# Softmax attention mixed with a spectral filter: a smaller third transform and a newly made order of work

## The chip, the cores and the metric

One core of a Trainium2 chip runs the whole program. The metric is the device time of one execution in microseconds (us). The engines are named TensorE (PE in the profile), VectorE (DVE), ScalarE (ACT), GpSimd (POOL) and SyncE (SP, which here only issues transfers).

## The reference

A token matrix x of 2048 x 448 goes through two branches, whose results are mixed by a gate of one number per token.

```python
g = sigmoid((x * gate_w).sum(-1, keepdims=True))
# branch a: 16 heads of 28
q, k, v = split(x @ wqkv)
a = softmax(q @ k.T / sqrt(28)) @ v @ wo
# branch b: a spectral filter over both axes
X = rfft2(x)                       # 2048 x 225 complex
b = irfft2(X * (w_r + 1j * w_i), s=(2048, 448))
out = g * a + (1 - g) * b
```

## The kernel before

**The stream of attention.** Heads are worked in 4 groups of 4, tokens of a group's queries in 4 blocks of 512: 16 chunks (`CHUNKS`). In each chunk 16 key tiles of 128 make a *pack* each: four score blocks of 128 x 512, one for each head, 1024 in all. A score block is one matmul on a strip of 32 rows of TensorE (`Emit.score`), so up to four run at once; the text calls such a group of concurrent matmuls a *cell*. ScalarE takes score blocks in pairs, from the two-bank tiles psA and psB in turn (`Emit.exp`, one ACTIVATE of 128 x 1024). VectorE takes whole packs from single banks psX: it makes the exponential's bit pattern with integer arithmetic, once (`bits`) and three times shifted (`shift`). Value cells (`value`) add into psV, four column strips of 32.

**The spectral branch** is done with matrix products beside the stream: `fft1` (over 128 token residues, result U), then `fft2`, which for each of 16 groups g does a second transform along the features (f2, result P2), a third one over the 16 remaining token steps (f3, result FX; its tables come by transfer into `tab`), the multiplication with the filter on GpSimd (the filter's rows come by transfer into Wf), and the first inverse one (i1). `fft3` and `final` finish it and add the output projection. A complex product in f3 is, before the change, one pass of 452 columns and two of 226 on full 128 partitions:

```python
self.mmc(bank[:, 0:452], tb[:, 0:128], p2[:, :], True, False)
self.mmc(bank[:, 0:226], tb[:, 128:256], p2[:, 226:452], False, False)
self.mmc(bank[:, 226:452], tb[:, 256:384], p2[:, 0:226], False, True)
```

`mmc` splits a product into four column strips of 32, which run at once.

**The order of the work** is written by a planner in the kernel itself (`Plan`), when the program is built. Each operation has an engine, a duration, dependencies and a priority; units of TensorE work have a place (`at`) and a due time in units of progress of the stream. The planner walks through time, takes for each engine the best operation that is ready, and puts out one list; each engine's queue is that list in order, and an engine waits at an instruction until what it depends on is done. `CFG` holds the weights, with own values for each of 72 stretches of progress (`seg`). `m_pe` and `m_bank` are reserves that the plan leaves between another engine's end and TensorE's start, and before a bank is used again. No duration in it is taken at run time. When TensorE has too little work the planner puts in cells on zeros (`zero`).

**The head** (`head`, `first`) transposes x block by block (xT, L1267 and L1274), projects the first key and query blocks, squares them on ScalarE (sq, L1302), adds a norm row by one matmul, and copies KT and QT (L1311, one KT copy at L1309 on ScalarE). Then the first scores are possible. The minimum of KT (`kmin`, L1277) is needed later, for a bound that the softmax uses in place of a maximum. **The tail** (`norm_last`, `final`) normalises the last chunk from psV on VectorE and finishes the last output tiles.

Of the kernel before, what the change touches and what calls it, by code (L numbers as in the profile page):

```python
# [18 lines left out]
FP = F + 1  # L19
# [22 lines left out]
def rfft_tables():  # L42
# [42 lines left out]
    tab = np.concatenate([CR, -CI, CI, CRt, -CIt, CIt, CRt, 0 * CR], axis=2)  # L85
# [32 lines left out]
class Op:  # L118
# [4 lines left out]
    passes = 1  # L123

# [40 lines left out]
class Plan:  # L165
# [152 lines left out]
    def step(self, eng, t):  # L318
# [7 lines left out]
        prog = self.progress()  # L326
        for o in lst:
            if o.start is not None:
                continue
            if o.ready > t:  # L330
                continue
# [149 lines left out]
    def tile_ready(self, tl):  # L481

        r = tl["ready"]
        for b in self.bank_of[tl["grp"]]:
            if self.owner[b] is not None and self.owner[b] != "stream":
                return None
            if not self.started or self.owner[b] is None:
                r = max(r, self.free_at[b])
        e = self.last_exp[tl["grp"]]
        if e is not None:  # L490
            if e.get("end") is None:
                return None
            r = max(r, e["end"] + self.cfg["l_pe"])
        return r
# [8 lines left out]
    def exp_dur(self, n):  # L503
        return 512 * n * 0.000833 + 0.055
# [14 lines left out]
    def exp_run(self, e, t):  # L519
# [3 lines left out]
        self.done(o, t, t + d + 0.11, t + d, "ACT")  # L523
# [84 lines left out]
    def d_sums(self, d):  # L608
# [16 lines left out]
        for v in range(1, 4):  # L625
            eng = "POOL" if (self.nd, v) in self.cfg["pool_shifts"] or (v == 1 and self.cfg["pool_every"] and self.nd % self.cfg["pool_every"] == 0) else "DVE"
            o = Op(eng, self.cfg["dve_shift"] if eng == "DVE" else self.cfg["pool_shift"],
                   (lambda e, v=v: self.em.shift(d["vslot"][v], d["slot"], v, e)), list(d["ops"]),
                   port=True, prio=self.cfg["prio_shift"], name="shift")
# [16 lines left out]
    def pe_step(self, t):  # L646
# [14 lines left out]
        def offer(score, kind, n, go, eff=1.0):  # L661
# [20 lines left out]
        for u in self.open:  # L682
            if u.pos < len(u.pe):
                o = u.pe[u.pos]
                if o.nwait == 0 and o.ready <= t:
                    offer(c["w_open"] - (c["w_due"] if u.due < prog else 0.0) - u.rush, o.kind, o.n, lambda u=u, o=o: self.unit_run(u, o, t), o.eff)
# [5 lines left out]
        if fb:  # L692
            nopen = ndue = 0
            for u in self.todo:
                if u.at > prog:
                    break
                if early and not u.rush:
                    continue
                o = u.pe[0]
                if o.nwait == 0 and o.ready <= t:  # L700
                    if u.due < prog:
                        ndue += 1
                    offer(c["w_new"] - (prog - u.at) * c["w_late"] - (c["w_due"] if u.due < prog else 0.0) - u.rush, o.kind, o.n, lambda u=u, o=o: self.unit_open(u, o, fb[-1], t), o.eff)
# [23 lines left out]
    def zero(self, t, kind, bank):  # L727
# [4 lines left out]
        x.emit = lambda: self.em.zero(kind, bank, first)  # L732
# [17 lines left out]
    def s_run(self, tl, t):  # L750
# [29 lines left out]
        while n > 0 and fb:  # L780
# [8 lines left out]
            n -= 1  # L789
        return True  # L790
# [55 lines left out]
    def unit_run(self, u, o, t):  # L846
# [8 lines left out]
    port_dep=6.0, last=((0, 2), (2, 2)), x_act=4, tiles=(2, 2), nring=20, nvar=10, nearly=5, l_pe=0.09, l_act=0.03, pe_lat=0.2, dma_issue=0.6,  # L855
    m_pe=0.2, m_bank=0.1, tol=0.1, max_ahead=9, nd_max=99, d_open=3, ahead=3, d_chunks=1, dve_op1=0.605, dve_shift=0.6, pool_shift=2.0,
    pool_shifts=(), pool_every=0, prio_op1=3, prio_shift=2.5, sh_max=4, d_urg=2, window=3.413, z_hard=3450, z_soft=3500, v2_at=2.0, v2_due=2.8,
    g_at=(0.9, 4.3, 8.0), g_due=1.0, w_pv=1.0, w_open=0.5, w_new=1.6, w_late=0.5, w_d=3, w_due=2, hungry=1.4, v_rush=2, x_rush=6, k_rush=5, q_rush=4,
    w_hungry=1, sw_pen=0, pv_min=1, ring_urg=2, d_first=True,
    seg={  # L860
        0: dict(d_open=4, w_hungry=0, z_hard=3550, w_open=1.2, tol=0.15),
        1: dict(d_open=4, w_hungry=0, z_hard=3550, w_open=1.2),
        2: dict(d_open=4, w_hungry=0, z_hard=3550, w_open=1.2, w_d=0.5, pv_min=2, tol=0),
        3: dict(d_open=4, w_hungry=0, z_hard=3550, w_open=1.2, w_due=4, z_soft=3800),
        4: dict(tol=0, d_open=2, prio_shift=3.5, z_hard=3350, d_urg=3, z_soft=4200),
        5: dict(tol=0, d_open=2, sw_pen=0.5, d_urg=0),
        6: dict(d_open=2),
        7: dict(d_open=2, w_d=2.2),
        8: dict(d_urg=3, pv_min=2, tol=0.06),
        9: dict(d_urg=3, pv_min=2, tol=0.06, z_hard=3350, d_chunks=0),  # L870
        10: dict(d_urg=3, pv_min=2, tol=0.06, w_due=1),
        11: dict(w_hungry=4),
        12: dict(tol=0.15, g_due=0.8, w_hungry=4, z_hard=3550),
        13: dict(tol=0.15, g_due=0.8, w_hungry=4, z_hard=3550, prio_shift=3),
        14: dict(tol=0.15, g_due=0.8, w_hungry=4, z_hard=3550, prio_shift=3, sw_pen=0.25),
        15: dict(tol=0.15, g_due=0.8, w_hungry=0, z_hard=3550, sw_pen=0.25, d_first=False, pv_min=3, hungry=1),
        16: dict(ahead=1, tol=0.15, g_due=0.8, w_hungry=0, z_hard=3550, sw_pen=0.25, d_first=False, pv_min=3, hungry=1, d_open=4),
        17: dict(ahead=2, tol=0.15, g_due=0.8, w_hungry=0, z_hard=3550, d_first=False, pv_min=3, hungry=1, prio_shift=3.5),
        18: dict(ahead=2, tol=0.15, g_due=0.8, w_hungry=0, z_hard=3550, d_first=False, pv_min=3, hungry=1, w_d=1, max_ahead=5),
        19: dict(ahead=2, tol=0.15, g_due=0.8, w_hungry=0, z_hard=3550, d_first=False, pv_min=3),  # L880
        20: dict(v2_due=3.1, w_pv=0.6, tol=0.15, g_due=0.8, w_hungry=0, z_hard=3550),
        21: dict(v2_due=3.1, hungry=4, w_pv=0.6, tol=0.15, g_due=0.8, w_hungry=0, d_first=False, d_open=4),
        22: dict(v2_due=3.1, hungry=4, w_pv=0.6, tol=0.15, g_due=0.8, w_hungry=0, d_first=False, d_open=4, ring_urg=8),
        23: dict(v2_due=3.1, hungry=4, w_pv=0.6, tol=0.15, g_due=0.8, w_hungry=4, prio_shift=3.5),
        24: dict(hungry=4, prio_shift=3.5, tol=0.15, g_due=0.8, w_hungry=0, w_due=4),
        25: dict(hungry=4, prio_shift=3.5, tol=0.15, g_due=0.8, w_hungry=0, w_due=4, d_open=2),
        26: dict(hungry=4, prio_shift=3.5, tol=0.06, g_due=0.8, w_hungry=0, w_due=4, d_open=2, sh_max=2),
        27: dict(hungry=4, prio_shift=3.5, tol=0.15, g_due=0.8, w_hungry=0, w_due=0.5, d_open=2, d_urg=3),
        28: dict(g_due=0.8, w_hungry=0, prio_shift=3.5, w_due=4, d_open=2, z_soft=4200, d_first=False),
        29: dict(g_due=0.8, w_hungry=0, prio_shift=3.5, w_due=4, d_open=2, z_soft=4200, d_first=False, sh_max=3),  # L890
        30: dict(g_due=0.8, w_hungry=0, prio_shift=3.5, w_due=4, z_soft=4200, d_first=False, sh_max=3),
        31: dict(g_due=0.8, prio_shift=3.5, w_due=4, w_hungry=0, z_soft=4200, d_first=False, sh_max=3, sw_pen=0.5, hungry=1),
        32: dict(g_due=0.8, prio_shift=3.5, w_due=4, w_hungry=2, z_soft=4200, d_first=False, sh_max=3, sw_pen=0.5, hungry=1),
        33: dict(g_due=0.8, prio_shift=3.5, z_soft=4200, d_first=False, sh_max=3, sw_pen=0.5, hungry=1, w_hungry=2, tol=0.06),
        34: dict(g_due=0.8, prio_shift=3.5, z_soft=4200, d_first=False, sh_max=3, w_hungry=0, d_urg=0, ahead=4),
        35: dict(g_due=0.8, prio_shift=3.5, z_soft=4200, d_first=False, w_hungry=2, d_urg=3),
        36: dict(d_urg=3, d_chunks=0, w_due=4, prio_shift=3.5, z_hard=3550, z_soft=4200, g_due=0.8, ring_urg=4, d_first=False, w_hungry=2),
        37: dict(d_urg=3, d_chunks=0, w_due=4, prio_shift=3.5, z_hard=3550, g_due=0.8, w_d=2.2),
        38: dict(d_urg=3, d_chunks=0, w_due=0.5, prio_shift=3.5, z_hard=3550, g_due=0.8, w_d=1.4, w_hungry=2),
        39: dict(d_urg=3, d_chunks=0, w_due=4, prio_shift=3.5, z_hard=3550, g_due=0.8, sh_max=3, pv_min=2, w_d=2.2, hungry=3),  # L900
        40: dict(prio_shift=3.5, d_urg=1, sh_max=3, pv_min=2, w_d=2.2, hungry=3),
        41: dict(prio_shift=3.5, d_urg=1, sh_max=3, pv_min=2, w_d=2.2, hungry=3, w_due=4, ring_urg=8, sw_pen=1),
        42: dict(prio_shift=3.5, d_urg=1, sh_max=3, pv_min=2, hungry=3, w_d=2.2),
        43: dict(d_urg=3, sh_max=3, pv_min=2, d_first=False, hungry=3, w_d=2.2),
        44: dict(d_urg=1, w_d=2.2, pv_min=2, z_soft=4200, z_hard=3250, w_late=1),
# [784 lines left out]
```

## Time and profile before

| | |
|---|---|
| median of 3 runs | 395.97 us (395.78 to 396.46) |
| the profiled execution | 396.53 us, of which its span from first to last instruction 394.4 us |
| granted TensorE clock, mean | 0.999 |
| TensorE busy | 382.2 us (97%), 5432 matmuls |
| ScalarE busy | 380.8 us (97%) |
| VectorE busy | 353.3 us (90%) |
| GpSimd busy | 131.2 us (33%) |
| transfers | 17.57 MB, mean 45 GB/s |

Busy time counts a record from its start to its end; records of one engine can overlap, and an instruction's record may hold its wait behind the one ahead. The time from one start to the next is therefore often the better price. A timeline row is: start in us, duration in us, engine, line, operation, output<-input, shapes, count, and in brackets the idle time before it and what ended that. A row of groups is: line, engine, operation, output<-input, shapes, count | busy us, mean ns of one | idle us before them. A row of the waits is: engine, output, line <- what it waited for: us in total, times, longest us.

### The profile page before, as it was taken

The page shows a single profiled execution, that of the slowest core. Times are in us where ns is not written, and L with a number is a line of the kernel's source. Part 1 is how long each engine was busy: PE and PEld are TensorE (multiplying, and loading weights), DVE is VectorE, ACT ScalarE, POOL GpSimd, SP SyncE. Part 2 cuts the span into 40 slices and gives each one's busy share as a digit, 9 for nine tenths or more (in the row PEclk, how much of TensorE's full clock was granted, in tenths as well). Part 3 has the DMA queues.
Part 4 walks back from the last instruction along what each step waited for, and adds up shares of the span by engine and source line. Part 5 has one row for each costly group of instructions (what it writes and reads, how often), then busy time and mean ns, then how long its engine had stood idle before and what let it go on. Part 6 is the DMA issues. An engine that isn't in the chain of part 4 may idle for free.

```text
span 394.4 us, 13102 instructions
## 1 busy us (share of the span) xinstructions
PE 382.2 (97%) x5432; PEld 134.9 (34%) x5432; DVE 353.3 (90%) x651; ACT 380.8 (97%) x421; POOL 131.2 (33%) x180
## 2 busy tenths in 40 slices
PE   7999999999999999999999999999999999999996
PEld 3544333223333333333433233332233333233333
DVE  3658989899899889989999899999999999999993
ACT  4899999999999999999999999999999999999994
POOL 3130513530530434553555254362343543001010
PEclk9999999999999999999999999999999999999999
DMA  8800012010201202121131200231010101010012
GB/s 243 180 29 5 4 18 56 16 30 3 62 12 47 55 9 67 41 59 50 28 84 40 69 3 30 67 87 38 3 28 3 31 2 30 24 51 27 27 52 71
DMA packets 24411, 17.57 MB, mean 45 GB/s; under 512 B 15731, under 2 KB 19872, under 8 KB 24352
## 3 DMA queue, kind: packets, MB, share of 16 engines
q1 hardware_dynamic: 23744, 16.55, 15.4%
q8 instruction: 42, 0.69, 0.7%
q10 hardware_dynamic: 608, 0.19, 0.3%
q14 instruction: 17, 0.14, 0.1%
HBM read 14.57 MB, written 1.97 MB: 42 GB/s over the span
## 4 chain that ended last, share of the span: by engine, by line
PE 59%; ACT 33%; issue 5%; DMA 1%; DVE 0%; SPq 0%; ACTq 0%
ACT P L963 30%; PE psX L1014 20%; PE psV L1014 18%; PE psA L1014 10%; PE psB L1014 10%; DMA xtok<-in_A_x_dram 1%; ACT VS L963 1%; ACT sq L1636 0%; PE psX L1267 0%; ACT sq L1302 0%; ACT xT L1274 0%; SPq L1169 0%; DVE KT L1311 0%; DVE QT L1311 0%; PE psV L1267 0%
## 5 line engine op out<-in xcount | busy, mean ns | idle before, releaser
L963 ACT ACTIVATE P<-psB 128x1024 bf16<-128x1024 f32 x196 | 218.4, 1114 | 0.3
L963 ACT ACTIVATE P<-psA 128x1024 bf16<-128x1024 f32 x196 | 217.8, 1111 | 0.3 <-ACT P L963 0.2
L992 DVE TENSOR_SCALAR VS<-psX 128x512 int16<-128x512 f32 x220 | 144.0, 683 | 10.6 <-PE psX L1014 9.7
L998 DVE TENSOR_SCALAR VS<-VS 128x2048 int16<-128x2048 int16 x165 | 107.5, 694 | 0.5
L1014 PEld LDWEIGHTS <-KT 32*128 32x128 bf16 x1040 | 47.2, 91 | 140.2 <-issue 136.7
L1014 PE MATMUL psB<-QT,KT 32*128 32x512 bf16 x402 | 78.4, 382 | 5.0 <-ACT P L963 4.0
L1014 PE MATMUL psA<-QT,KT 32*128 32x512 bf16 x402 | 78.8, 383 | 1.2 <-ACT P L963 0.6
L1014 PE MATMUL psV<-VS,Vb 128*32 128x512 bf16 x900 | 79.7, 385 | 0.0
L1014 PE MATMUL psV<-P,Vb 128*32 128x512 bf16 x784 | 72.0, 384 | 0.0
L1014 PE MATMUL psX<-QT,KT 32*128 32x512 bf16 x220 | 71.1, 383 | 0.2
L1521 POOL TENSOR_TENSOR t<-FX,Wf 128x452 bf16<-128x452 f32 x32 | 31.8, 1014 | 68.0 <-DVE FX L1518 34.0
L1014 PEld LDWEIGHTS <-Vb 128*32 128x32 bf16 x1684 | 33.0, 94 | 54.5 <-issue 50.0
L1601 POOL TENSOR_TENSOR xtok<-osb,RB 128x512 bf16<-128x512 f32 x12 | 15.3, 1275 | 38.6 <-DMA RB<-rgd 23.8
L1575 POOL TENSOR_TENSOR UZ<-tab 128x225 bf16<-128x225 f32 (+1 forms) x32 | 17.9, 583 | 29.5 <-DVE VS L998 20.7
L1249 POOL TENSOR_TENSOR sq<-QT 128x512 bf16<-128x512 bf16 x16 | 16.6, 1041 | 29.8 <-PE psX L1014 12.1
L1529 POOL TENSOR_TENSOR t<-t,t 128x226 bf16<-128x226 bf16 x32 | 18.1, 583 | 14.5 <-DVE VS L998 13.1
L1014 PE MATMUL psX<-xT,Wk 112*32 112x512 bf16 x256 | 20.5, 383 | 0.0
L1249 POOL TENSOR_TENSOR sq<-KT 128x512 bf16<-128x512 bf16 x12 | 12.5, 1041 | 21.6 <-DVE KT L1239 12.6
L1014 PE MATMUL psX<-xT,Wq 112*32 112x512 bf16 x240 | 19.7, 383 | 0.0
L1014 PE MATMUL psX<-Wv,xT 112*32 112x113 bf16 (+1 forms) x512 | 19.1, 262 | 0.0
L1014 PEld LDWEIGHTS <-xT 112*32 112x32 bf16 (+1 forms) x576 | 10.6, 95 | 10.4 <-issue 8.1
L1546 DVE CAST Qf<-psX 113x512 bf16<-113x512 f32 x16 | 10.9, 683 | 1.5 <-PE psX L1014 1.3
(107 smaller groups left out, 322.2 us busy)
## 6 DMA issues: line engine op xcount, KB each, us to landing
tab<-c_tab SPq DMA_DIRECT2D x16, 256.0 KB
RB<-rgd SPq DMA_DIRECT2D x60, 64.0 KB
xtok<-in_A_x_dram SPq DMA_DIRECT2D x4, 448.0 KB
out_dram<-ost SPq DMA_DIRECT2D x6, 224.0 KB
rs<-osb SPq DMA_DIRECT2D x60, 2.0 KB
Wf<-in_B_w_r_dram SPq DMA_DIRECT2D x31, 28.1 KB
Wf<-in_B_w_i_dram SPq DMA_DIRECT2D x31, 28.1 KB
Qf<-in_A_wqkv_dram SPq DMA_DIRECT2D x2, 294.0 KB
```

The source lines that it names most:

```text
L963: k.nc.scalar.activation(out=out, in_=k.psS[e["grp"]][:, 0:n, :], func=ACT.Exp, scale=LN2_128)
L992: k.nc.vector.tensor_scalar(out=k.VS[:, slot, 512 * h:512 * h + 512], in0=bank, scalar1=float(BITS0), scalar2=BITS_MIN, op0=ALU.add, op1=A ...
L998: k.nc.vector.tensor_scalar(out=k.VS[:, dst, :], in0=k.VS[:, src, :], scalar1=float(SHIFTS[v - 1]), scalar2=None, op0=ALU.add)
L1014: self.nc.tensor.matmul(out, lhsT=lhsT, rhs=rhs, start=start, stop=stop, skip_group_check=True, **kw)
L1249: (self.nc.vector if e == "DVE" else self.nc.gpsimd).tensor_tensor(out=sq[:, :], in0=src, in1=src, op=ALU.mult)
L1521: ts.append(pl.op("POOL", 1.07, lambda e, i=i, q=q: nc.gpsimd.tensor_tensor(out=self.t12[i][q][:, :].rearrange("p (r f) -> p r f", r=2), i ...
L1529: (nc.vector if e == "DVE" else nc.gpsimd).tensor_tensor(out=t1[:, FP * q:FP * q + FP], in0=t1[:, FP * q:FP * q + FP], in1=t2[:, FP - FP * ...
L1546: self.o_q.append(u.use("DVE", 0.61, lambda bank, e, g=g: nc.vector.tensor_copy(out=self.Qv[0:FC, :, :, 8 * g:8 * g + 8], in_=bank[0:FC, : ...
L1575: nc.gpsimd.tensor_tensor(out=z, in0=a, in1=b, op=ALU.subtract if q else ALU.add)
L1601: prev = pl.op("POOL", 1.3, lambda e, G=G, j=j: nc.gpsimd.tensor_tensor(out=self.ON[G][:, 512 * j:512 * j + 512], in0=self.osb[:, :], in1= ...
```

## The change

- **Third transform.** f2 now writes real and imaginary part of half a group each onto the two halves of the 128 partitions (h = 0, 1), so P2 holds two halves of 226 columns, each with 64 rows of real and 64 rows of imaginary part; f3 multiplies each half by a table of 128 rows, two passes of 226 columns. The tables (`rfft_tables`) are put in that order and shrink from 1024 to 768 columns; the output rows of a group are reordered ([6, 7, 0, ..., 5]), and with them the filter's rows, which are loaded in more pieces.
- **First transform's copies.** U is stored with the 16 token steps innermost; one copy of 512 elements writes it where two of 256 did.
- **Head.** The minimum of the first KT block stands behind QT's copy; the condition on later transposes is another; three xT copies may be ScalarE's where four could.
- **Plan.** Most durations get new values (exponential 0.904 for 0.908 us, a copy 0.602 for 0.605 or more), ScalarE's results count as ready 0.05 to 0.07 us later, `m_pe` is 0.1 for 0.2, `m_bank` 0 for 0.1; rushed units may pass the limit ahead of the next scores by `late`; nearly all of `seg` is new. The zero cells use `ost` as long as the constants are not loaded.
- **Not active.** `pieces=0`, `pc_hold=0` and `p_shift=99` leave the new strip-wise projection and the shifts on GpSimd unused.

```diff
 rfft_tables
-    tab = np.concatenate([CR, -CI, CI, CRt, -CIt, CIt, CRt, 0 * CR], axis=2)
+    order = np.array([6, 7, 0, 1, 2, 3, 4, 5])
+    out = (16 * order[:, None] + a).reshape(128)
+    base = base[:, order]
+    halves = []
+    for h in range(2):
+        row = (8 * t + 4 * h + np.arange(4)[:, None]).reshape(64)
+        col = out[64 * h:64 * h + 64]
+        cr, ci = (v[:, row][:, :, col] for v in (CR, CI))
+        halves += [np.concatenate([cr, -ci], axis=1), np.concatenate([ci, cr], axis=1)]
+    CRt, CIt = CRt[:, out], CIt[:, out]
+    tab = np.concatenate(halves + [CRt, -CIt, CIt, CRt], axis=2)
...
 Plan
-            free, end = t + d, t + d + o.tail
+            free, end = t + d, t + d + o.tail + (0.07 if eng == "ACT" else 0.0)
...
-            r = max(r, e["end"] + self.cfg["l_pe"])
+            r = max(r, e["end"] + self.cfg["l_exp"])
...
-        return 512 * n * 0.000833 + 0.055
+        return 512 * n * 0.000833 + 0.051
...
-        self.done(o, t, t + d + 0.11, t + d, "ACT")
+        self.done(o, t, t + d + 0.16, t + d, "ACT")
...
-            if t + cost + (self.SW if kind != "row" else 0.0) > lim:
+            if t + cost + (self.SW if kind != "row" else 0.0) > lim + late:
                 return
+            if late:
+                score -= 30.0
...
 CFG
-    m_pe=0.2, m_bank=0.1, tol=0.1, ... dve_op1=0.605, dve_shift=0.6, pool_shift=2.0,
+    m_pe=0.1, m_bank=0.0, tol=0.1, ... dve_op1=0.602, dve_shift=0.6, pool_shift=2.2,
+    p_shift=99, pieces=0, pc_keep=1, pc_hold=0, late=0.1, ...
-    x_act=4, ...
+    x_act=3, l_exp=0.04, ...
     seg={ ... 72 entries, nearly all new ... }
...
 tiles
-        self.U = self.UZ[:, :].rearrange("p (c g t e) -> p c g t e", c=NC, g=NT, t=NT)
+        self.U = self.UZ[:, :].rearrange("p (c x t) -> p c x t", c=NC, t=NT)
...
 head
-                u.mm(tr, ..., deps=[self.d_x[b], self.d_cst, sel[0] if (b, cp) == (1, 1) else sel[1] if b > 1 else None])
+                u.mm(tr, ..., deps=[self.d_x[b], self.d_cst, sel if 2 * b + cp > 2 else None])
...
-            mins.append(pl.op("DVE", 0.6, ... tensor_reduce kmin ..., [k], prio=-2))
             if b == 0:
                 self.q_ready[0] = self.first(1, 0, "q0", self.selrow, 2)
                 pl.marks["q0"] = self.on_q0
-                sel = [self.sq_use[0], self.sq_use[2]]
+                sel = self.sq_use[2]
+            mins.append(pl.op("DVE", 0.6, ... tensor_reduce kmin ..., [k] if b else [k, self.q_ready[0]], prio=-2))
...
 fft1
-                    for t in range(2):
-                        nc.vector.tensor_copy(out=self.U[0:n, 2 * c:2 * c + 2, :, 2 * tq + t, :],
-                                              in_=bank[0:n, 256 * t:256 * t + 256].rearrange("p (f g e) -> p f g e", f=2, g=NT))
-                self.o_u.append(u.use("DVE", 0.7, ev))
+                    nc.vector.tensor_copy(out=self.U[0:n, 2 * c:2 * c + 2, :, 2 * tq:2 * tq + 2].rearrange("p f x t -> p f t x"),
+                                          in_=bank[0:n, :].rearrange("p (t f x) -> p f t x", t=2, f=2))
+                self.o_u.append(u.use("DVE", 0.602, ev))
...
 fft2
-            for c in range(4):
-                n = 128 if c % 2 else 97
-                u.mm(... self.mmc(bank[:, FP * (c // 2):FP * (c // 2) + FP], U of g, self.Bd[0:n, c, :], ...), n=FP, ...)
+            for h in range(2):
+                for rb in range(2):
+                    def f2(bank, g=g, h=h, rb=rb):
+                        n = 128 if rb else 97
+                        for o in range(4):
+                            f = o // 2
+                            w = self.U[0:n, 2 * rb + f, 8 * g + 4 * h:8 * g + 4 * h + 4, :].rearrange("p e t -> p (e t)")[:, 32 * (o % 2):32 * (o % 2) + 32]
+                            self.mm(bank[32 * o:32 * o + 32, FP * h:FP * h + FP], w, self.Bd[0:n, 2 * f + rb, :], rb == 0, rb == 1, pos=(0, 32 * o))
+                    u.mm(f2, n=FP, kind="bg", ...)
...
             def f3(bank, i=i):
                 tb, p2 = self.tab[i], self.P2[i]
-                self.mmc(bank[:, 0:452], tb[:, 0:128], p2[:, :], True, False)
-                self.mmc(bank[:, 0:226], tb[:, 128:256], p2[:, 226:452], False, False)
-                self.mmc(bank[:, 226:452], tb[:, 256:384], p2[:, 0:226], False, True)
-            p2use[i] = u.mm(f3, n=452, count=2, kind="bg", deps=[ev, loads[g][0]])
+                for q in range(2):
+                    for o in range(4):
+                        h = o // 2
+                        c = 128 * h + 64 * q + 32 * (o % 2)
+                        self.mm(bank[32 * o:32 * o + 32, FP * q:FP * q + FP], tb[:, c:c + 32], p2[:, FP * h:FP * h + FP], True, True, pos=(0, 32 * o))
+            p2use[i] = u.mm(f3, n=226, count=2, kind="bg", deps=[ev, loads[g][0]])
```

More of the change, by code (lines that the diff above doesn't have):

```diff
@@ L123 @@
     passes = 1
+    strips = None
     def __init__(self, eng, dur, emit, deps, port=False, prio=5, tail=0.1, name="", alt=None, unit=None):
@@ L326, in step @@
         prog = self.progress()
+        many = eng == "POOL" and sum(1 for o in lst if o.name == "shift" and o.start is None and o.ready <= t) >= self.cfg["p_shift"]
         for o in lst:
@@ L329, in step @@
                 continue
-            if o.ready > t:
+            if o.ready > t or eng == "POOL" and o.name == "shift" and not many:
                 continue
```

283 lines of the change are left out of this document (172 added, 111 removed).

## The prediction

> **What bounds the kernel now.** I read the page first, then ScalarE's and TensorE's timelines, then the waits. The page:
>
> ```profile
> span 394.4 us, 13102 instructions
> ...
> PE 382.2 (97%) x5432; PEld 134.9 (34%) x5432; DVE 353.3 (90%) x651; ACT 380.8 (97%) x421; POOL 131.2 (33%) x180
> ...
> PE 59%; ACT 33%; issue 5%; DMA 1%; DVE 0%; SPq 0%; ACTq 0%
> ...
> L963 ACT ACTIVATE P<-psB 128x1024 bf16<-128x1024 f32 x196 | 218.4, 1114 | 0.3
> ```
>
> Two engines stand at 97%, and the chain that ended last changes between them: neither can be sped up alone. ScalarE's work is fixed: 402 exponentials of two banks each (196 and 5 from psA, as many from psB), and both programs hold 402, with 220 score blocks left to VectorE in both. So the question is how densely the exponentials stand, where the first begins, and what comes behind the last. ScalarE's timeline:
>
> ```profile
> 12.87 1.02 ACT L963 ACTIVATE VS<-psA 128x1024 bf16<-128x1024 f32 x1 [1.10 <-PE psB L1014]
> ...
> 14.70 0.60 ACT L1302 ACTIVATE sq<-psX 128x512 bf16<-128x512 f32 x1
> 15.18 1.04 ACT L963 ACTIVATE VS<-psA 128x1024 bf16<-128x1024 f32 x1
> ...
> 16.98 0.72 ACT L1309 ACTIVATE KT<-psX,onef 128x512 bf16<-128x512 f32 x1
> 17.55 0.64 ACT L1302 ACTIVATE sq<-psX 128x512 bf16<-128x512 f32 x1
> ...
> 221.98 1.04 ACT L963 ACTIVATE P<-psB 128x1024 bf16<-128x1024 f32 x1
> ...
> 227.40 1.12 ACT L963 ACTIVATE P<-psB 128x1024 bf16<-128x1024 f32 x1
> ...
> 384.77 1.03 ACT L963 ACTIVATE P<-psB 128x1024 bf16<-128x1024 f32 x1
> ```
>
> The records overlap (a record of 1.1 us contains its wait behind the one ahead), so starts are what counts. From 221.98 to 227.40 lie six exponentials: 5.42/6 = 0.904 us each when nothing is missing. From the first start, 12.87, to the last, 384.77, are 371.9 us and 401 steps; 401 x 0.904 = 362.5. Between them ScalarE also does three squares (15.18 - 14.70 = 0.48 each), one KT copy (17.55 - 16.98 = 0.57) and two small operations (about 0.1 each): 2.2 us. The remainder, 371.9 - 362.5 - 2.2 = 7.2 us, is time in which the next scores were not there. It comes in small pieces; it is what a better order can win in the middle. Outside lie 12.9 us of head and 394.4 - 384.8 = 9.6 us of tail.
>
> What makes scores late is TensorE, whose timeline shows the prices:
>
> ```profile
> 150.63 0.57 PE L1014 MATMUL psX<-P,tab 128*32 128x452 bf16 x12
> 151.02 0.39 PE L1014 MATMUL psV<-VS,Vb 128*32 128x512 bf16 x4
> 151.34 0.39 PE L1014 MATMUL psB<-QT,KT 32*128 32x512 bf16 x2
> ...
> 152.21 0.39 PE L1014 MATMUL psA<-QT,KT 32*128 32x512 bf16 x2
> 152.44 0.37 PE L1014 MATMUL psX<-QT,KT 32*128 32x512 bf16 x1
> ```
>
> Again by starts: a cell (up to four concurrent matmuls of 512 columns on different strips) costs 152.44 - 152.21 = 0.23 us if the next has the same tiling, and 151.34 - 151.02 = 0.32 us if the tiling changes from column strips to row strips; so about 0.22 us for the columns and 0.10 for a change. The third transform is the first row: 151.02 - 150.63 = 0.39 us.
>
> **Part by part.** *Third transform (f3).* Real and imaginary part now stand on the two partition halves, so the four-term product needs one pass over 452 columns where it took one of 452 and two of 226: 904 columns become 452, for each of 16 groups. Half of 0.39 us less any change of tiling is about 0.19 us; 16 x 0.19 = 3.0 us of TensorE. The fore-running transform (f2) writes the halves directly and keeps 64 cells of 226 columns: nothing. The tables shrink from 1024 to 768 columns: DMA only.
>
> *The new order.* I counted cells and changes of tiling in the instruction lists of both built programs. All columns together: 275.3 us to 272.7 us at full rate (f3's 3.0 less, four more filler cells on zeros, 0.9, and 0.4 less for score cells that now ride in more common cells). Changes of tiling: 775 to 756, 19 x 0.10 = 1.9 us. From the first to the last score pair, TensorE's listed work falls from 348.8 to 344.5 us: 4.3 us less in a stretch in which ScalarE needs 362.5.
>
> How much of 4.3 us reaches the end? Not all: TensorE's list is shorter than ScalarE's in the middle already, and what delays ScalarE is locally crowded cells. A measure for that: over every two successive score pairs (1.81 us of ScalarE) I summed the listed TensorE work beyond 1.81 us, halved because pairs overlap: 11.4 us before, 9.8 after; over single intervals, beyond 0.904, 22.1 and 19.1. Both shrink by 14%. The measured 7.2 us of late scores, reduced by 14%, give 1.0. The largest part of it is in the last fifty exponentials, where both the crowding and the measured lateness of before are largest, so I take 1.1 us. Bounds: 4.3 us gained (every freed microsecond comes through), and below nothing, since the plan's slack is cut too (a rival, below).
>
> *Head.* The rows from which it follows:
>
> ```profile
> 10.26 0.75 DVE L1311 TENSOR_SCALAR KT<-psX,onef 128x512 bf16<-128x512 f32 x1 [2.49 <-ACT sq L1302]
> ...
> 10.65 0.40 PE L1014 MATMUL psX<-sq,cst 128*32 128x512 bf16 x4
> ...
> 10.98 2.40 SPq L1169 DMA_DIRECT2D Wf<-in_B_w_r_dram  x3
> 11.05 0.69 DVE L1277 TENSOR_REDUCE kmin<-KT 128x1 f32<-128x512 bf16 x1
> 11.07 0.61 PE L1267 MATMUL psX<-cst,xtok 128*112 128x128 bf16 x8
> 11.51 0.61 PE L1267 MATMUL psV<-cst,xtok 128*112 128x128 bf16 x8
> 11.65 0.74 DVE L1311 TENSOR_SCALAR QT<-psX,onef 128x512 bf16<-128x512 f32 x1
> 12.31 0.68 DVE L1274 COPY xT<-psX 112x1024 bf16<-112x1024 bf16 x1
> 12.45 0.39 PE L1014 MATMUL psA<-QT,KT 32*128 32x512 bf16 x2 [0.33 <-DVE QT L1311]
> ```
>
> The minimum of KT stood ahead of QT's copy; now it stands behind. QT can start at about 11.05 where it started at 11.65, a gain of 0.60 on VectorE. What is late next is TensorE: 16 transposes still stand ahead of the first scores, and they cannot begin before KT's bank is read (11.07); they end near 11.95, plus a change of tiling 12.05. So the first scores go from 12.45 to 12.05: -0.40 us, not -0.60.
>
> Moved with it: ScalarE loses one xT copy that stood ahead of the first exponential (in its wait, nothing) and the KT copy, -0.57 us on its path; VectorE takes both, about 0.6 us each, behind QT's copy and so off the chain until the third exponential. The price: 24 transposes stand between the first and second round of scores instead of none; eight need the bank that the xT copy frees. With KT, QT, minimum and xT in a row, that copy ends near 13.0; two sets of eight transposes (0.44 each by 11.07 to 11.51) lead to 13.9, the change to 14.05, the third exponential to 14.05 + 0.42 (12.87 - 12.45) = 14.5. It was due 2 x 0.90 after the first at 12.47, so 14.28: +0.2 us. Head in all: -0.40 - 0.57 + 0.2 = -0.8 us.
>
> *First transform's copies.* 32 copies of 256 elements become 16 of 512 that write single elements 32 bytes apart. The rows of VectorE's groups:
>
> ```profile
> L1472 DVE CAST UZ<-psX 97x256 bf16<-97x256 f32 (+1 forms) x32 | 11.8, 417 | 0.1
> L1546 DVE CAST Qf<-psX 113x512 bf16<-113x512 f32 x16 | 10.9, 683 | 1.5 <-PE psX L1014 1.3
> ...
> L1205 DVE MEMSET Vb<- 128x192 bf16 x1 | 0.2, 218 | 0.6 <-issue 0.6
> ...
> L1198 DVE MEMSET Wk<- 128x64 bf16 x1 | 0.1, 112 | 0.2 <-issue 0.2
> ```
>
> At the price of Qf's copy (same element count, runs of eight) the new copies cost 10.9 us against 11.8: 0.9 less on an engine off the chain, taken at nothing. Do scattered single elements cost more? The two fills write single elements 64 bytes apart: (218 - 112)/128 = 0.83 ns for each further element, no more than a copy's 683/512 = 1.33. So I take the price of Qf's copy; the upper bound is a doubled element, about 0.53 us more per copy, 8.5 us in all.
>
> [...]
>
> *SyncE.* The rows of the filter halves are cut in three or four pieces where they were two or three: 66 Wf transfers become 98, at 0.8 us of issue each (three took 2.40 us in the head's rows) 26 us over a span of 394 on a queue that mostly waits. Behind them stand the normalisers' transfers; these have whole chunks of time. Four of the 32 stand in the head, ahead only of transfers that wait for later work. Nothing, up to 0.5 us if one normaliser comes late.
>
> *Tail.* Behind the last score pair:
>
> ```profile
> 384.19 0.39 PE L1014 MATMUL psB<-QT,KT 32*128 32x512 bf16 x2
> ...
> 386.36 0.39 PE L1014 MATMUL psV<-P,Vb 128*32 128x512 bf16 x4
> ...
> 389.22 0.36 PE L1014 MATMUL psX<-Bd,xT 128*32 128x448 bf16 x4
> ...
> 390.54 0.36 PE L1014 MATMUL psX<-Bd,xT 128*32 128x448 bf16 x4
> ```
>
> Before, 6 value cells and 26 of 448 columns (0.19 us each) follow; after, 4 and 30. The last value cell can start 1.67 us behind the score pair (it needs the last exponential) where it was 386.36 - 384.19 = 2.17. But 26 cells then follow, 26 x 0.19 = 4.94, against 22. VectorE's normaliser needs 389.22 - 386.36 = 2.86 us and is covered by 14 cells, just. The end on TensorE: 1.67 + 0.22 + 4.94 = 6.83 us behind the last pair against 390.54 + 0.19 - 384.19 = 6.54: +0.3 us.
>
> **The sum.** On the profiled execution's own time, 396.53 us (span 394.4 and 2.1 around it): 396.53 - 0.8 - 1.1 + 0.3 = 394.9. That execution was 0.56 above the median of the runs, 395.97, so for a median I say **394.4 us**, 1.6 less.
>
> **The rivals.** *All of TensorE's saving comes through* (4.3 for 1.1): 391.2 us. For it: both engines at 97%, and the new plan's price of an exponential, 0.904 us, is the row's (0.908 before). Against it: TensorE's listed 348.8 us already leave 23 of the 371.9 us free, and 7.2 us of scores are late all the same.
>
> *The gain is eaten by waits: no change.* The plan's reserve from another engine to TensorE is halved (0.2 to 0.1 us) and that for a freed bank is 0. TensorE takes its queue in order, so a result 0.05 us later than planned stops all that follows. If late scores stay 7.2 us and 0.6 is lost at new waits, 395.97 - 0.8 + 0.3 + 0.6 = 396.1.
>
> *Slower by those waits.* The place is the pair of scores waiting for the exponential that frees its bank:
>
> ```profile
> PE psB L1014 <- ACT P L963: 4.0, 13, 0.5
> ...
> PE psA L1014 <- ACT P L963: 0.6, 3, 0.2
> ```
>
> Now 4.6 us over 16 times. If a tenth of the 402 pairs waits 0.1 us more and each wait delays its exponential, 4 us are added: 396.1 + 4 x 0.5 = 398 if half of them have no cover, 400 if none has. It decides when these rows pass about 7 us in total.
>
> *Scattered writes at double price.* The copies stand between 37 and 70 us:
>
> ```profile
> L1472 DVE CAST UZ<-psX x32: 414/415/425, 37.1 to 69.6; 97x256 bf16<-97x256 f32 x16, 128x256 bf16<-128x256 f32 x16
> ```
> ```profile
> 40.00:60.00 20.00, 20.00 (x328) 7.60 (x319) 18.63 (x47) 20.00 (x24) 7.30 (x26) 1.00 0.09 10
> ```
>
> VectorE (the third column of busy time) is free for 1.4 us in 20 there, 2.3 in 33. Of 8.5 us more, 6.2 find no room, and the value cells, which TensorE takes in order, wait for VectorE: 394.4 + 6.2 = 400.6. It decides when the new copies pass 0.9 us. [...]
>
> *The change does not do what it says*: the lists show f3 with 128 matmuls of 226 columns and none of 452; nothing is left of this one.
>
> **How the numbers follow.** Forecast (393.3 to 395.3) 0.48; all comes through, or most (391 to 393.3), 0.17; no change 0.18; slower by waits 0.13; scattered writes 0.04. Range 391.6 to 397.4: it leaves out the far end of the first rival and most of the slower ones. A measurement here can tell about 0.2%, 0.8 us, from no change. Faster by more (below 395.2): 0.46 + 0.17 = 0.63; same: 0.02 + 0.18 = 0.20; slower 0.17.
>
> **What would show it.** f3's start to the next cell near 0.20 us; first exponential near 12.5; KT no longer on ScalarE; UZ copies at 0.68 us; from first to last exponential 371.9 - 0.57 + 0.2 - 1.1 = 370.4 us; 9.9 us behind the last start. Wrong if the waits for psA and psB grow past 7 us, if UZ's copies cost over 0.9, or if first to last exponential falls below 369 (then the freed work was worth more than the crowding said).

## The result and the profile after

The changed kernel takes 425.71 us (median of 6 runs, 424.68 to 429.2) where the kernel before takes 396.22 beside it: a ratio of 1.076 (95% interval 1.072 to 1.081). One run of before took 534.41 us; the ratios, here and below, leave it out, with other runs that lie over 1.5% above the fastest of their kernel. The forecast was 394.4, the range 391.6 to 397.4; it is wrong by 31 us and in sign. The page of its profiled execution (427.38 us, span 425.6), the lines that answer to those shown of before:

```profile
span 425.6 us, 13044 instructions
...
PE 400.1 (94%) x5384; PEld 137.3 (32%) x5384; DVE 378.3 (89%) x637; ACT 383.0 (90%) x419; POOL 130.5 (31%) x180
...
ACT  4899556475899999999999999999999999999994
...
PEclk9979659685899999999999999999999999999999
...
ACT 48%; PE 31%; DVE 10%; issue 9%; DMA 1%; SPq 0%; DVEq 0%; ACTq 0%
...
L1034 ACT ACTIVATE P<-psB 128x1024 bf16<-128x1024 f32 x196 | 216.0, 1102 | 15.5 <-PE psB L1088 10.2
...
L1551 DVE CAST UZ<-psX 97x512 bf16<-97x512 f32 (+1 forms) x16 | 37.1, 2363 | 2.8 <-PE psX L1088 2.8
```

ScalarE is no longer dense, but only in the first third: its digits fall to between 4 and 8 from about 43 to 117 us. VectorE, 0% of the chain before, is 10% of it now. In all but one of these slices the clock of TensorE (PEclk) is no longer full. And the copies to UZ (L1551) cost 2363 ns each, not 683. The windows of 20 us (busy time of PE, PEld, DVE, ACT, POOL, then clock, DMA share and GB/s):

```profile
40.00:60.00 20.00, 14.87 (x163) 4.84 (x161) 16.59 (x20) 11.51 (x13) 5.41 (x24) 0.69 0.01 2
60.00:80.00 20.00, 15.63 (x202) 5.08 (x200) 19.00 (x20) 12.87 (x13) 3.09 (x3) 0.84 0.20 35
80.00:100.00 20.00, 16.79 (x178) 4.75 (x178) 19.08 (x18) 12.79 (x13) 4.10 (x5) 0.67 0.03 8
100.00:120.00 20.00, 19.48 (x196) 4.75 (x192) 14.13 (x25) 15.34 (x18) 5.61 (x7) 0.78 0.06 16
120.00:140.00 20.00, 19.81 (x291) 6.93 (x287) 19.30 (x37) 20.00 (x23) 6.34 (x7) 1.00 0.10 27
```

From 40 to 120 us ScalarE is busy for 52.5 of 80 us (before: all 80); from 120 us on it is full. The last copy starts at 98.8 us, so the loss outlasts the copies by some 20 us: from 100 to 120 us TensorE is busy for 19.48 of 20 us, but at a clock of 0.78, and ScalarE for 15.34. The rows of the copies and TensorE's waits:

```profile
L1551 DVE CAST UZ<-psX x16: 2298/2344/2608, 39.7 to 98.8; 97x512 bf16<-97x512 f32 x8, 128x512 bf16<-128x512 f32 x8
```
```profile
PE psX L1088 <- DVE UZ L1551: 10.0, 10, 1.6
PE psB L1088 <- ACT P L1034: 4.5, 15, 0.5
...
PE psA L1088 <- ACT P L1034: 0.6, 3, 0.2
```

The waits that the prediction watched (psA and psB for ScalarE) stand at 5.1 us where they were 4.6. The largest new one is for UZ: 10.0 us directly, a third of the loss. Two questions follow: what makes such a copy cost 2.34 us, and what makes the rest, when TensorE waits for the copies only 10 us. And a third: what would the change be worth without this?

### The profile page after: what moved, and what is told of

Its sections match the earlier page's. It is cut to its first block, busy times and chain, and to the rows that moved or that the text cites. A ratio compares the mean times of both kernels' runs of the same rounds, so it can differ in the third digit from the quotient of the medians.

```text
span 425.6 us, 13044 instructions
## 1 busy us (share of the span) xinstructions
PE 400.1 (94%) x5384; PEld 137.3 (32%) x5384; DVE 378.3 (89%) x637; ACT 383.0 (90%) x419; POOL 130.5 (31%) x180
## 4 chain that ended last, share of the span: by engine, by line
ACT 48%; PE 31%; DVE 10%; issue 9%; DMA 1%; SPq 0%; DVEq 0%; ACTq 0%
ACT P L1034 47%; PE psX L1088 12%; PE psV L1088 9%; DVE UZ L1551 6%; PE psB L1088 5%; PE psA L1088 4%; DVE VS L1066 2%; DVE VS L1072 1%; DMA rs<-osb 1%; PE psX L1347 1%; ACT VS L1034 1%; SPq L1243 0%; DVE osb L1679 0%; ACT sq L1382 0%; DVE Vb L1477 0%
## 5 line engine op out<-in xcount | busy, mean ns | idle before, releaser
L1034 ACT ACTIVATE P<-psB 128x1024 bf16<-128x1024 f32 x196 | 216.0, 1102 | 15.5 <-PE psB L1088 10.2
L1088 PE MATMUL psB<-QT,KT 32*128 32x512 bf16 x402 | 81.3, 396 | 6.2 <-ACT P L1034 4.5
L1088 PE MATMUL psV<-VS,Vb 128*32 128x512 bf16 x900 | 82.1, 401 | 1.5 <-DVE Vb L1493 1.4
L1088 PE MATMUL psA<-QT,KT 32*128 32x512 bf16 x402 | 81.2, 395 | 0.9 <-ACT P L1034 0.6
L1088 PE MATMUL psX<-QT,KT 32*128 32x512 bf16 x220 | 73.2, 393 | 3.7 <-DVE UZ L1551 2.1
L1088 PE MATMUL psV<-P,Vb 128*32 128x512 bf16 x784 | 74.8, 397 | 0.2 <-DVE osb L1679 0.2
L1551 DVE CAST UZ<-psX 97x512 bf16<-97x512 f32 (+1 forms) x16 | 37.1, 2363 | 2.8 <-PE psX L1088 2.8
L1088 PE MATMUL psX<-xT,Wk 112*32 112x512 bf16 x256 | 23.0, 419 | 1.1 <-DVE UZ L1551 1.1
L1088 PE MATMUL psX<-Wv,xT 112*32 112x113 bf16 (+1 forms) x512 | 20.9, 278 | 0.0
L1088 PE MATMUL psX<-cst,xtok 128*32 128x256 bf16 (+1 forms) x144 | 11.2, 323 | 6.8 <-DVE UZ L1551 6.8
```

The source lines that it names most:

```text
L1034: k.nc.scalar.activation(out=out, in_=k.psS[e["grp"]][:, 0:n, :], func=ACT.Exp, scale=LN2_128)
L1088: self.nc.tensor.matmul(out, lhsT=lhsT, rhs=rhs, start=start, stop=stop, skip_group_check=True, **kw)
L1551: nc.vector.tensor_copy(out=self.U[0:n, 2 * c:2 * c + 2, :, 2 * tq:2 * tq + 2].rearrange("p f x t -> p f t x"), in_=bank[0:n, :].rearrange ...
```

## The experiments

**The copy alone.** A kernel that only makes copies of 512 elements to bf16, each form six times, the distance between single elements in SBUF varied; it leaves all of the computation out.

> No part of the reference's computation: VectorE and ScalarE copies by themselves, six of each kind, nothing beside them. Theory A (single elements 32 bytes apart are dear to write): 512 elements from PSUM into bf16 take 0.68 us at stride 1 and about 2.3 us at stride 16, and the copy of the changed kernel in its own pattern 2.3 us. Theory B (the order in which PSUM is read is what costs): stride 16 from a plain read 0.68 us, the pattern of the changed kernel 2.3 us. Theory C (VectorE was held up by other engines' traffic): all of them 0.68 us. Under A the strides in between (2, 4, 8) show where it begins; the fills at stride 16 and 32 stay at 0.83 ns an element.

Groups by line. From PSUM: L55 step 1, L57 step 2 (4 bytes), L59 step 4 (8 bytes), L63 step 16 (32 bytes), L67 the change's own pattern, L69 the same elements with the two neighbours in the inner loop. L89 and L91 are fills at steps 16 and 32, L95 is ScalarE's copy at step 16.

```profile
L95 ACT CAST big<-p 128x512 bf16<-128x512 f32 x6 | 13.8, 2293 | 0.2
L63 DVE CAST big<-p 128x512 bf16<-128x512 f32 x6 | 13.8, 2293 | 0.2
L59 DVE CAST big<-p 128x512 bf16<-128x512 f32 x6 | 7.7, 1290 | 0.2
...
L69 DVE CAST big<-p 128x512 bf16<-128x512 f32 x6 | 4.2, 692 | 0.2
L55 DVE CAST big<-p 128x512 bf16<-128x512 f32 x6 | 4.1, 691 | 0.2
...
L91 DVE MEMSET big<- 128x512 bf16 x6 | 2.9, 485 | 11.2 <-issue 11.2
```
```profile
L67 DVE CAST big<-p 128x512 bf16<-128x512 f32 x6 | 14.0, 2326 | 0.2
```

A copy of single 2-byte elements costs 0.69 us side by side, 0.73 at 4 bytes, 1.29 at 8 and 2.29 at 32 bytes; step 8 (16 bytes) gave 2.42. And L69 shows the way out: the same 512 elements at the same addresses cost 0.69 if two neighbours are written in a row.

The scattered *fill* has a record of 0.485 us at steps 16 and 32 alike, and such records are what the prediction took its price from. But ahead of each of them the engine stands idle and waits for nothing that the profile shows ("issue"). The timeline, first two fills of 512 neighbours, then two scattered ones:

```profile
22.00 0.48 DVE L31 MEMSET srcf<- 128x512 f32 x1
22.59 0.48 DVE L32 MEMSET p<- 128x512 f32 x1
...
142.72 0.48 DVE L89 MEMSET big<- 128x512 bf16 x1 [1.77 <-issue]
144.98 0.48 DVE L89 MEMSET big<- 128x512 bf16 x1 [1.77 <-issue]
```

From one start to the next a fill of neighbours takes 0.59 us and a scattered one 2.26 (2.34 at step 32): the same price as the copies. The record of a fill shows only the number of its elements (485 ns for 512, in either pattern), and the rest, 1.77 us at step 16, stands as idle time ahead of it. That is where the prediction went astray, for its own two rows had this idle time in their last column (0.6 and 0.2 us). In the timeline of before:

```profile
2.63 0.70 DVE L1204 MEMSET Vb<- 128x768 bf16 x1 [0.42 <-issue]
3.95 0.22 DVE L1205 MEMSET Vb<- 128x192 bf16 x1 [0.62 <-issue]
```

From the end of the first, 3.33, to the end of the second, 4.17, are 0.84 us for 192 scattered elements, 4.4 ns each; by this estimate 512 of them would take 2.2 us.

**Where the price comes from.** The same with other sources and types, the order fixed by dependencies.

> No part of the reference's computation: VectorE copies of 512 elements by themselves, in a fixed order, by source (PSUM fp32, SBUF fp32, SBUF bf16), output type and step. If the price belongs to a 2-byte element alone in its 32 bytes, every source has 2.3 us at step 16 and pairs have 0.69; if it belongs to reading PSUM while writing so, the SBUF sources stay near 1.2 us; if it belongs to bytes between elements, fp32 at steps of 4 and 8 elements (16 and 32 bytes) also has 2.3 us.

L67 and L89: step 16 from PSUM and from fp32 in SBUF; L85: fp32 elements written 32 bytes apart; L71: pairs of bf16, pair to pair 64 bytes.

```profile
L67 DVE CAST big<-p 128x512 bf16<-128x512 f32 x6 | 13.8, 2293 | 0.2
...
L89 DVE CAST big<-srcf 128x512 bf16<-128x512 f32 x6 | 7.4, 1240 | 0.2
...
L85 DVE COPY bigf<-p 128x512 f32<-128x512 f32 x6 | 6.4, 1073 | 0.2
...
L71 DVE CAST big<-p 128x512 bf16<-128x512 f32 x6 | 4.2, 692 | 0.2
```

The price hangs on the width too: 32 bytes apart, 4-byte elements cost 1.07 us and 2-byte ones 2.29 from PSUM and 1.24 from SBUF; pairs of 2-byte ones (4 bytes) from PSUM cost 0.69, no more than side by side.

**The scattered copies alone, in the kernel before.** Its tables are permuted to suit; the order of its queues and all else stay.

```
- self.UZ[:, :].rearrange("p (c g t e) -> p c g t e", ...)   # two copies of 256
+ self.UZ[:, :].rearrange("p (c x t) -> p c x t", ...)       # one of 512, singles at 32 bytes
```

> The kernel before with the scattered copies alone (U with the token steps innermost, one copy of 512, the third transform's table rows permuted); its own plan, which books 0.70 us for them. Theory A: the copies take 2.3 us, 16 x (2.34 - 0.67) = 27 us more on VectorE, the clock falls in this stage, the time is 415 to 428 us. Rival (the new plan is at fault): 396 to 399 us.

423.94 us (median of 4, 418.52 to 426.81; ratio 1.063, 1.055 to 1.070). By the medians this one edit alone loses 27.7 of the 29.5 us that the change loses, by the ratios 24.8 of 30.2: most of the loss, in the order of before.

**The changed kernel without scatter.** Two copies of 256 in runs of four, U laid out accordingly, the same order of all queues:

```
+ for t in range(2):
+     nc.vector.tensor_copy(out=self.U[0:n, 2*c:2*c+2, :, :, 2*tq+t, :]...,  # runs of 4
```

> The changed kernel with U stored in runs of four elements (two copies of 256 each, as before the change), the third transform's table rows permuted to match; the planner's durations and so every queue's order stay as in the changed kernel. Theory A (the scattered copies are the whole loss): the copies take 0.42 us each, the granted clock is back at 0.99, the time is 391 to 395.5 us. Rival (the cut slack of the plan costs too): 397 us or more, with waits of psA and psB for the exponential over 7 us.

398.0 us (ratio 1.0046, 1.0028 to 1.0064): 27.7 us less than the changed kernel, but not all is back. The time is the rival's, its sign is not there: the waits for psA and psB are 5.4 us. The granted clock was 0.991 in every run. Windows of one microsecond show where:

```profile
24.00:25.00 1.00, 0.87 (x17) 0.58 (x16) 0.61 (x1) 1.00 (x2) 0.85 (x2) 1.00 0.07 25
25.00:26.00 1.00, 0.76 (x10) 0.35 (x9) 0.00 (x0) 1.00 (x2) 0.73 (x1) 0.78 0.07 25
26.00:27.00 1.00, 1.00 (x36) 0.81 (x34) 0.00 (x0) 1.00 (x3) 0.00 (x0) 0.50 0.07 25
...
32.00:33.00 1.00, 1.00 (x15) 0.23 (x11) 0.42 (x2) 0.39 (x1) 0.00 (x0) 0.80 0.00 0
```

For seven microseconds the clock is halved (0.50), and ScalarE, full until 28 us, is idle for 2.0 of the next 5 us, where before it was never idle. What stands ahead of it in TensorE's timeline:

```profile
24.10 0.35 PE L1088 MATMUL psX<-cst,KT 128*128 128x4 bf16 x8
24.58 0.39 PE L1088 MATMUL psB<-QT,KT 32*128 32x512 bf16 x2
24.91 0.35 PE L1088 MATMUL psX<-cst,KT 128*128 128x4 bf16 x8
25.50 0.59 PE L1088 MATMUL psA<-QT,KT 32*128 32x512 bf16 x2 [0.24 <-ACT P L1034]
```

Sixteen matmuls of four columns within 1.2 us. Before, at a clock of 1.00 throughout, four of the same sixteen start at 23.24 us, eight from 23.74 on and the last four after longer work at 27.31:

```profile
23.74 0.35 PE L1014 MATMUL psX<-cst,KT 128*128 128x4 bf16 x8
...
27.31 0.25 PE L1014 MATMUL psX<-cst,KT 128*128 128x4 bf16 x4
```

That this is the cause is a guess so far; the version with four fills below tests it. The changed kernel has the same dip in the third slice of its clock (the 7, from 21 to 32 us), before the copies begin.

**The right price in the plan.** The planner was told 0.602 us for the copies; here 2.27, the copies still scattered.

```
- self.o_u.append(u.use("DVE", 0.602, ev))
+ self.o_u.append(u.use("DVE", 2.27, ev))
```

> The changed kernel with its scattered copies, but the plan books 2.27 us for each where it booked 0.602: the copies cost the same, the order is made for them. If the loss is VectorE's added work itself (27 us on an engine that was 90% busy), the time is 405 to 425 us. If most of it is TensorE waiting in its queue behind a copy that the plan thought short, and the clock that falls with it, the time is below 405 us and the granted clock above 0.98.

416.42 us (414.7 to 419.21; ratio 1.053, 1.046 to 1.059), its two fastest runs, 414.7 and 414.81, at a clock of 1.000. So the loss splits: 18.5 us stay with an order that knows the price and a full clock; about 11 us came from the order that didn't know it and the clock that fell with it. The new order is not only a matter of places: the planner now gives VectorE 204 score blocks for 220 and ScalarE 410 exponentials for 402, 8 x 0.904 = 7.2 us of work, and the last exponential starts 13.7 us from the end of the span, not 9.8.

**Pairs.** The changed kernel with the copy's loops in another order, the same addresses, the same queues:

```
- out=self.U[...].rearrange("p f x t -> p f t x"), in_=bank.rearrange("p (t f x) -> p f t x", t=2, f=2)
+ out=self.U[...],                               in_=bank.rearrange("p (t f x) -> p f x t", t=2, f=2)
```

> The changed kernel with one edit: the copies of the first transform go through their 512 elements in another order, the two neighbouring token steps first, so that each 32-byte step gets a pair of elements one behind the other. Layout, all other instructions and every queue's order are the changed kernel's. Theory A (a single element in each 32 bytes is what is dear): 0.69 us a copy, as alone, and the time of the version with runs of four or 0.5 us better, 397.0 to 398.2 us, with the clock still falling once near 25 us. Rival (the pairs are cheap only when nothing else runs): copies over 1 us, 400 us or more.

```profile
L1551 DVE CAST UZ<-psX 97x512 bf16<-97x512 f32 (+1 forms) x16 | 10.8, 683 | 1.2 <-PE psX L1088 1.2
```

The copies cost 683 ns, the figure that the prediction had. 397.94 us median of 12 runs (ratio 1.0032, 1.0013 to 1.0052), and the time goes with the clock: 394.39, 395.47 and 395.9 us at 1.000, 397.3 to 398.8 for most of the others, at 0.987 to 0.996. The longest run, 406.69 us at 0.966, is the profiled one; its clock is at 0.50 a second time, from 211 to 231 us (a mean of 0.90 from 200 to 300), behind a wait of 0.69 us of TensorE for GpSimd. No run tests whether that wait is the cause.

**Pairs, and the clock held.** Four matmuls of 448 columns on zeros among the sixteen small ones:

```
+ self.mm(bank[:, 64:512], self.ost[:, 0, 0:128], self.ost[:, 0, :], True, True)   # once for each four
```

> The version before it with four matmuls on zeros (448 columns, 0.19 us each) put between the sixteen 4-column matmuls of the key weights, near 24 to 25 us, into the unused columns of the same bank; all else in the same order. Theory C (the new order lets TensorE's activity fall too low near 25 us and the clock is halved for 7 us): the clock stays at 1.00, ScalarE's stalls in 20 to 40 us fall from 3.0 to about 0.6 us, the time is 394.5 to 396 us. Rival (the stalls there have another cause, such as the cut slack): no change or 0.7 us slower than the version before it.

395.57 us (394.82 to 397.2, 12 runs; before 396.04): ratio 0.9995 (0.9983 to 1.0006), clock 0.996 to 1.000. So the four fills take the loss of the clock away, and this is the change as the prediction understood it. From the first exponential's start, 11.81, to the last, 383.66, are 371.85 us; without 362.5 and 1.65 for the three squares and two small operations, 7.7 us of late scores remain, 0.5 more than before. One wait behind the head is new, TensorE for GpSimd's products with the filter, and ScalarE's next exponential starts 1.79 us behind the one before it (205.41 and 207.20):

```profile
206.49 0.29 PE L1088 MATMUL psX<-tab,t 128*32 128x256 bf16 x4 [0.73 <-POOL t L1617]
```
```profile
207.20 1.02 ACT L1034 ACTIVATE P<-psB 128x1024 bf16<-128x1024 f32 x1 [0.72 <-PE psB L1088]
```

**Is TensorE's saved time worth anything?** In that kernel 452 columns of real data are multiplied ahead of each third transform, into the bank that it then overwrites: the 3.0 us are given back.

```
+ self.mmc(bank[:, 0:452], tb[:, 0:128], p2[:, :], True, True)
```

> The changed kernel with pairs and four fills (395.57 us), with 452 columns of real data multiplied ahead of each third transform into the same bank and overwritten by it: it gives back to TensorE the 16 x 0.19 = 3.0 us that the change took away, in the changed order. By the prediction's crowding measure (9.8 us rise to 11.5 with these cells) 7.7 us of late scores should grow by about 1.1 to 1.3: 396.8. If each microsecond of TensorE comes through: 398.5. If the time of TensorE between score pairs is mostly spare, as the middle of the list suggests: 395.4 to 396.0, no change that can be measured.

395.24 us (395.11 to 395.86, 11 runs) against 395.95 before: ratio 0.9983 (0.9974 to 0.9992), the only version whose interval lies below 1. In sum, three microseconds more for TensorE cost nothing; late scores are 371.83 - 362.5 - 1.65 = 7.7 us as without them. But in the two profiled runs two things cancel. From the 101st exponential's start to the 201st's are 91.58 us without the added cells and 92.26 with them, 0.7 more; from there to the 301st's 92.68 and 91.98, 0.7 less, for the wait for GpSimd is not in this run (with runs of four and with pairs it is there too, 0.7 us each). So in this order, as far as one profile of each shows, the saved 3.0 us are worth about 0.7, and a wait that comes with them takes that back.

**The third transform in the old order.** The queues of the kernel before, with the new f2 and f3, pairs, and the filter rows in more pieces.

> The kernel before with the new second and third transform, their tables, the pair copies and the filter's loads alone: plan, durations and every queue's order are those of the kernel before, which still books 904 columns for the third transform. It measures what 3.0 us less on TensorE bring by themselves. If freed TensorE time comes through, 393.2 us; if it is lost in local crowding, as the prediction's 14% said for the whole, 395.2 to 396.2 us.

400.42 us (ratio 1.011, 1.008 to 1.014), clock 0.982 to 1.000. TensorE's timeline and windows of 5 us of its profiled run:

```profile
251.66 0.37 PE L1024 MATMUL psX<-Bd,UZ 128*32 128x226 bf16 x8
253.74 0.61 PE L1024 MATMUL psA<-QT,KT 32*128 32x512 bf16 x2 [1.72 <-DMA QT<-brow]
```
```profile
249.25 2.00 SPq L1505 DMA_DIRECT2D Wf<-in_B_w_i_dram  x3
251.35 2.32 SPq L1179 DMA_DIRECT2D QT<-brow  x4
```
```profile
250.00:255.00 5.00, 3.29 (x56) 1.34 (x56) 3.81 (x6) 3.22 (x4) 2.62 (x4) 0.86 0.09 22
255.00:260.00 5.00, 5.00 (x44) 1.10 (x40) 2.58 (x5) 3.54 (x4) 0.00 (x0) 0.50 0.13 39
```

Three pieces of each filter half where there were two push the transfers to QT from 249.43 to 251.35 us; TensorE waits 1.72 us for them, and then the clock is halved (0.50) for more than ten.

**The same, with QT's transfers ahead of the filter's last half** on SyncE's queue, in the two places where they stood behind it. Nothing else is different.

> The kernel before in its own order with the new second and third transform, the copies in pairs and the filter rows in more pieces, as in the run of the third transform alone (400.42 us), but on SyncE's queue the normaliser's transfers to QT now stand ahead of the three pieces of the imaginary filter half, in the two places where they stood right behind them. In that earlier run TensorE waited 1.72 us for the last of these transfers at 252 us (first issue at 251.35 where the kernel before has 249.43), and the clock was 0.50 from about 254 to 267 us. Theory A, the queue: the wait starts it and the half clock follows from it. Then no wait for QT's rows over 0.3 us, transfers from about 249.7, clock 1.00 in all or nearly all runs, and a time of 395.0 to 396.0, that is what three microseconds less of TensorE work are worth by themselves, 0 to 1 us. Theory B, the missing work: with 3 us less for TensorE its activity falls below what holds the clock, wait or no wait. Then the clock still drops between 240 and 280 us, mean 0.98 to 0.99, and the time stays at 399 to 401.

```profile
247.17 2.12 SPq L1529 DMA_DIRECT2D Wf<-in_B_w_r_dram  x3
249.86 2.36 SPq L1202 DMA_DIRECT2D QT<-brow  x4
252.27 2.10 SPq L1529 DMA_DIRECT2D Wf<-in_B_w_i_dram  x3
```

396.66 us (396.02 to 397.96, 11 runs; ratio 1.0018, 1.0008 to 1.0027), clock 1.000 in most runs: the queue, not the missing work, made the 400. And in the old order the third transform brings nothing either: its start to the next cell falls from 0.49 to 0.37 us in the median (to 0.30 in the new order), but the time lies 0.7 us above the kernel before, and above the 395.0 to 396.0 expected. Part of it is a wait that the kernel before doesn't have, TensorE for VectorE's copy of P2:

```profile
193.48 0.48 PE L1024 MATMUL psX<-Bd,UZ 97*32 97x226 bf16 x12 [0.46 <-DVE P L1557]
```

## Why the prediction was wrong, point by point

- **The copies to UZ: the step that failed.** "So I take the price of Qf's copy", because the records of two fills (218 and 112 ns) seemed to show that single elements cost nothing more. The fills pay too: the 0.6 and 0.2 us of idle time in the same two rows belong to them. A copy took 2.34 us where 0.68 was taken and 1.21 (0.68 + 0.53) was the upper bound; the 0.53 was the author's estimate, and the rows of before give the same ((683 - 417)/256 = 1.04 ns for a further element, 512 times). The rival of scattered writes had the mechanism, the place and the deciding point (0.9 us), but a chance of 0.04 and a third of the price. Its own sum with the measured price: 16 x (2.34 - 0.68) = 26.6, less 2.3 us of room on VectorE, is 24.3; 394.4 + 24.3 = 418.7, against 416.42 when the plan knew the price. That the two are close is partly luck: in that run part of VectorE's work went to ScalarE, and the tail grew by 4 us.
- **The clock was taken as given.** No term of the sum let TensorE's granted clock change. In the changed kernel it is part of the other 11 us: behind the last copy ScalarE still loses 4.7 us from 100 to 120 us, with TensorE busy at 0.78 (how much more is the clock's was not separated from the order). In most runs with pairs it cost 2 to 3 us, which four fills took away (the medians are 397.94 and 395.57 us).
- **The gain in the middle, -1.1 us, came where it was looked for and was lost elsewhere.** The last fifty steps take 46.02 us with pairs and fills, where they took 46.93: 0.9 us won. But with the clock held, late scores are 7.7 us in all, not 6.1: single late exponentials, the one after 73.71 us (0.6 late) and the one at the wait for GpSimd (0.9), cost more than that. The measure of crowding summed the list and had no term for a new wait. What the second rival foresaw (the gain is eaten by waits, 0.6 us at new ones, 396.1) is close to what the pairs with fills show, 395.57.
- **Right by their rows:** f3's saving (0.49 us to the next cell before in the median, its change of tiling included, 0.30 after: -0.19); the copies in pairs at 0.68; KT off ScalarE; the waits for psA and psB, 5.1 us in the changed kernel against the limit of 7. The head's order: the first exponential stands 6.28 us behind the first copy of xT where it stood 6.66, so -0.38 for -0.40 (it starts at 12.10, not 12.5, because x came 0.39 earlier in this execution); the third exponential is late by 0.23 for 0.2:

```profile
13.02 1.02 ACT L1034 ACTIVATE VS<-psB 128x1024 bf16<-128x1024 f32 x1
14.15 1.02 ACT L1034 ACTIVATE VS<-psA 128x1024 bf16<-128x1024 f32 x1
```
```profile
415.84 1.03 ACT L1034 ACTIVATE P<-psB 128x1024 bf16<-128x1024 f32 x1
```

- **The tail:** the last exponential starts at 415.84 of 425.6, 9.76 us from the end, where 9.9 was said and 9.63 stood before.
- **SyncE: nothing** holds in the changed order (the waits of TensorE's matmuls there show none for QT's rows), where the plan has placed the transfers anew; in the old order two more pieces ahead of QT's transfers cost some 4 us (400.42 against 396.66). The prediction's bound, 0.5 us, was too low for a transfer that TensorE waits for.

What stays open: why a scattered copy from SBUF takes 1.24 us, about half of what one from PSUM or a scattered fill takes; how the 11 us divide between order and clock; and what makes up the rest of the 0.7 us in the old order with the new f3, beside that wait of 0.46.

## What to carry to other kernels

Take a price from a row of the same operation, source and type, and from one start to the next: the records of the fills hid three quarters of their price in the idle time ahead of them. The order of loops in one copy, at the same addresses, was worth 28 us here. Time taken off an engine that is only busy is worth little until shown otherwise (0.7 of 3.0 us here, and a new wait took it back); and look at the clock behind a short gap or a bunch of small matmuls on a busy TensorE: here it was at 0.50 for more than ten microseconds behind a wait of 1.72 us, which cost some 4 us in all (400.42 against 396.66), and for seven behind sixteen small matmuls within 1.2 us, which cost 2.4 (397.94 against 395.57). An added transfer is costed by what is queued behind it (here QT's transfers, for which TensorE waited those 1.72 us).

## What the runs showed of the hardware

- A copy of 512 single bf16 elements, 16, 32 or 64 bytes apart, took 2.29 to 2.42 us from PSUM on VectorE, the same on ScalarE at 32 bytes (2293 ns both), 1.29 at 8 bytes, 1.24 from SBUF at 32 bytes; in pairs, 32 or 64 bytes from pair to pair, 0.69. A copy that reads at 32 bytes and writes side by side in SBUF took 0.60. A fill of 512 single elements, 32 or 64 bytes apart, took 2.26 to 2.34 us from start to start, though its record says 0.485.
- The clock fell to 0.50 for about seven microseconds behind sixteen four-column matmuls within 1.2 us, where the longest gap on TensorE was 0.24 us, and for more than ten behind one wait of 1.72 us. With four matmuls on zeros among the sixteen the mean clock was 0.996 to 1.000, and with QT's transfers ahead, so without the wait, 0.994 to 1.000. How long a wait or how many small matmuls it takes, no run shows.
